# Nine unused tiles that shift the others in SBUF, in a fused attention and bilinear-GLU block

## The chip, the cores and the metric

One NeuronCore of a Trainium2 chip runs the whole program. The metric is the device time of one execution in microseconds; a kernel's time is the median of several executions.

## The reference, cut to what matters

```python
# S = 2048 tokens, D = 576, H = 32 heads of Dh = 18, F = 4608, everything float32
def _A_ref(x, wq, wk, wv, wo):            # 32 query heads, one shared key and value head
    q = (x @ wq).reshape(B, S, H, Dh).transpose(0, 2, 1, 3)
    k, v = x @ wk, x @ wv
    p = softmax(einsum("bhqd,bkd->bhqk", q, k) * Dh ** -0.5)
    return einsum("bhqk,bkd->bhqd", p, v).transpose(0, 2, 1, 3).reshape(B, S, H * Dh) @ wo
def _B_ref(x, w_gate, w_up, w_down):      # bilinear GLU, no nonlinearity
    return ((x @ w_gate) * (x @ w_up)) @ w_down
h  = x + _A_ref(layernorm(x), wq, wk, wv, wo)
h2 = h + _B_ref(layernorm(h), w_gate, w_up, w_down)
```

## The kernel before, in words

The 2048 tokens are four blocks of 512 (`NB`, `TB`). Almost every product is built from float32r matmuls: an operand is split into a high part and the rest (`split`: a cast on one engine and a subtraction on another), and a product is the sum of high by high, high by low and low by high.

*First stage, to about 300 us.* `keys_values` normalises x, transposes it into `XT` (nine chunks of 512 columns per block), and makes keys (`kT`), values (`V`) and the queries. Queries go through DRAM (`q_dram`) and come back four heads at a time as a tile `q`.

*Attention.* `pair` issues one pair of score matmuls (line 593): keys of 128 positions are the weights, 512 queries are the moving operand; the two matmuls of a pair use the partitions 0 to 55 and 64 to 119 at the same time. ScalarE takes the exponential of the pair's 1024 columns into a tile `P` (line 594). `flush` then issues the four matmuls of `P` with `V` (line 598), which are plain float32 and appear as eight instructions.

*Feed-forward stage, from about 360 us.* `ffn(b)` runs over 36 slices of the hidden width for each token block. A slice has 27 pairs of matmuls (line 986): the gate and the up product run at the same time on the two halves of the partitions. Their weights are slices of `ws`, 128 columns each, and their moving operand is a chunk of `X`, 512 columns. While attention for a later block is still to be done (token blocks 0 and 1), a score pair is put in front of every fourth pair (`j % 4 == 0`) and the outputs are called `pg` and `pu`. In token blocks 2 and 3 no scores are left and the output is called `gu`. Every second slice is followed by `down` (line 946): 42 matmuls whose weights are 128-column slices of `room` and whose moving operand is 288 columns of `wdo`; they form a seven-product scheme over two hidden slices.

*Loads.* `load_w` loads the weights of a slice into `wr`, 4608 bytes per partition. `split_w` (line 852) splits them into one of two `ws` tiles of 9216 bytes and loads the slice after next. `load_wd` loads `wdo`.

*Where tiles lie in SBUF.* Pools lie one after another in the order in which they are opened, a pool's tiles in the order of their first use, and each size is rounded up to 32 bytes. So a tile's address is the sum of what is in front of it. In this kernel all chunk steps along the operands of lines 593, 946 and 986 are multiples of 128 bytes, so that all matmuls of a line see the same remainder of their address by 128. TensorE executes its instructions in the order in which the program lists them (`manual_schedule`), and no order depends on an address.

Of the kernel before, what the change touches and what calls it, by code (L numbers as in the profile page):

```python
# [17 lines left out]
F32 = mybir.dt.float32  # L18
# [7 lines left out]
P = 128  # L26
# [28 lines left out]
class Block:  # L55
# [796 lines left out]
    def split_w(self, n):  # L852
        if n < NF * NB:
            r = self.wr.pop(n)
            w = self.ws[n] = self.wp.tile([P, 2, 9, P], F32R, tag="ws", bufs=2, name=f"ws{n}")
            self.split(w[:, 0], w[:, 1], r, self.nc.gpsimd.tensor_copy)
            self.load_w(n + 2)

# [297 lines left out]
    def run(self):  # L1156
        from contextlib import ExitStack
        tc = self.tc
        self.q_dram = tc.dram_tile([NB, H * DH, 3, TB], F32, name="q_dram")
        self.wd_dram = tc.dram_tile([NC, P, 7, 2, HD], F32, name="wd_dram")  # L1160
        self.m_dram = tc.dram_tile([NB, 2, H, TB], F32, name="m_dram")
        self.known, self.n_mx = [0] * NB, 0
        self.tqs, self.p2 = [], None
        self.begin(True)
        with ExitStack() as st:
            pool = lambda name, bufs, **k: st.enter_context(tc.tile_pool(name=name, bufs=bufs, **k))
            cp, self.lp, self.hp = pool("const", 1), pool("ln", 2), pool("resid", 2)
            self.qp, self.pp, self.op, self.otp = pool("q", 2), pool("P", P_BUFS), pool("o", 1), pool("oT", 1)
            self.ps, self.w0 = pool("ps", 1, space=PSUM), pool("w0", 3)
            self.C = cp.tile([P, C_W], F32, name="C")  # L1170
            self.ident = self.C[:, C_ID:C_ID + P]
            self.kT = cp.tile([P, S], F32R, name="kT")
            self.V = cp.tile([P, NT, 32], F32, name="V")
            self.G = cp.tile([P, 64], F32R, name="G")
            self.mx = cp.tile([H, 8], F32, name="mx")
            st.enter_context(tc.manual_schedule())
            with tc.tile_pool(name="p0q", bufs=1) as self.p0q:
                self.wq_h = self.p0q.tile([P, 5, 28 * DH], F32R, name="wq_h")
                self.wq_l = self.p0q.tile([P, 5, 28 * DH], F32R, name="wq_l")
                self.kvq = self.p0q.tile([P, NB, TB], F32, name="kvq")  # L1180
                self.XT = [self.p0q.tile([P, 9, TB], F32R, tag=f"XT{b}", name=f"XT{b}") for b in range(NB)]
                with tc.tile_pool(name="qb", bufs=2) as self.qb:
                    def rest():
                        for b in range(1, NB):
                            yield from self.queries(b)
                    others = rest()
                    self.keys_values(others)
                    self.cast = self.dve.tensor_copy
                    live, due = True, 0.0
                    while live:  # L1190
                        if self.n_pair >= WO_FROM and not self.wo_r0:
                            for c in range(3):
                                self.load_wo_0(c)
                        self.pair()
                        due += RATE
                        while due > 0 and live:
                            z = next(others, None)
                            live = z is not None
                            due -= z or 0
                        self.pair()  # L1200
                        self.run_aux(1)
                        self.flush(len(self.pend) - 1)
            self.wp, self.hh, self.p2 = pool("w", 2), pool("hid", 4), pool("P2", 1)
            self.blocks()
            self.guard()
# [141 lines left out]
```

## Time and profile before

| | |
|---|---|
| median of 3 runs | 2293.43 us (2293.05 to 2294.3) |
| profiled execution: its time, its span | 2291.9 us, 2290.4 us |
| TensorE (PE) busy | 2268.7 us, 99% of the span |
| weight loads (PEld) busy | 1599.6 us, 70% |
| ScalarE (ACT), VectorE (DVE), GpSimd (POOL) busy | 1436.5, 1180.3, 681.3 us |
| granted TensorE clock | 0.999 |

The span runs from the first to the last instruction; the profiled execution's time is 1.5 us longer than its span, and 1.5 us shorter than the median of the runs. In the rows of the profile "64\*128 64x512" are the rows and columns of the array that a matmul uses and the shape of its moving operand. In the view of one line's instructions, three numbers with slashes are the minimum, the median and the maximum duration of one instruction in ns. A matmul's duration is longer than the distance to the next one, since matmuls are pipelined.

### The profile page before, as it was taken

Reading aid. Unit: us, or ns where it says so; the run is one execution under the profiler, and the core shown is the slowest. Engines: PE = TensorE matmul, PEld = TensorE weight load, DVE = VectorE, ACT = ScalarE, POOL = GpSimd, SP = SyncE. Lnnn points to the kernel's source line nnn. Section 1 sums busy time; section 2 is a strip of 40 time slices with the busy share of each in tenths; the row PEclk is TensorE's granted clock in tenths of the full one; section 3 lists DMA queues with packets and bytes.
Section 4 is the critical chain, followed back from the end, with each engine's and each line's share of the span. In section 5 each row is a group of like instructions: output and inputs, shape, how many; then the busy total and the mean of one; then the engine's idle time right before and its main releaser. Section 6 shows DMA issues by size and latency. Waiting matters only on the chain.

```text
span 2290.4 us, 45926 instructions
## 1 busy us (share of the span) xinstructions
PE 2268.7 (99%) x18114; PEld 1599.6 (70%) x18114; DVE 1180.3 (52%) x2152; ACT 1436.5 (63%) x1877; POOL 681.3 (30%) x856
## 2 busy tenths in 40 slices
PE   8999999999999999999999999999999999999998
PEld 6333346677777767677767677777767788888987
DVE  8232435565656567343434355444444476566665
ACT  5889887776676666767666767667677623232332
POOL 4000003455554444122221222222122233333342
PEclk9999999999999999999999999999999999999999
DMA  5222304434333344533333343633333354655553
GB/s 176 81 75 73 111 30 136 148 139 151 136 122 128 136 159 137 207 115 122 113 114 105 125 128 125 192 125 120 98 118 118 120 173 171 213 171 171 179 186 109
DMA packets 127129, 306.75 MB, mean 134 GB/s; under 512 B 17553, under 2 KB 17681, under 8 KB 126265
## 3 DMA queue, kind: packets, MB, share of 16 engines
q1 hardware_dynamic: 126905, 303.73, 39.8%
q8 instruction: 145, 2.38, 0.4%
q14 instruction: 79, 0.65, 0.1%
HBM read 233.76 MB, written 55.67 MB: 126 GB/s over the span
## 4 chain that ended last, share of the span: by engine, by line


## 5 line engine op out<-in xcount | busy, mean ns | idle before, releaser
L594 ACT ACTIVATE P<-s 128x1024 f32<-128x1024 f32 x1024 | 1024.0, 1026 | 271.4 <-PE s L593 189.6
L986 PE MATMUL pg<-X,ws 64*128 64x512 f32 x2592 | 706.9, 391 | 0.0
L986 PE MATMUL pu<-X,ws 64*128 64x512 f32 x2592 | 706.7, 391 | 0.1
L986 PEld LDWEIGHTS pg<-X,ws 64*128 64x128 f32 x2592 | 480.2, 186 | 75.9 <-issue 1.2
L986 PEld LDWEIGHTS pu<-X,ws 64*128 64x128 f32 x2592 | 478.1, 186 | 19.1 <-DVE h L751 1.0
L598 PE MATMUL acc<-P,V 128*32 128x512 f32 x4096 | 487.9, 598 | 0.0
L593 PE MATMUL s<-q,kT 56*128 56x512 f32 x2048 | 455.3, 423 | 5.2 <-ACT P L594 3.3
L946 PEld LDWEIGHTS y<-wdo,room 128*128 128x128 f32 x2856 | 386.9, 188 | 46.7 <-issue 44.2
L946 PE MATMUL y<-wdo,room 128*128 128x288 f32 x2856 | 403.7, 300 | 0.0
L953 ACT COPY tmp<-y 128x288 f32<-128x288 f32 x408 | 162.7, 399 | 330.8 <-PE y L946 313.2
L593 PEld LDWEIGHTS s<-q,kT 56*128 56x128 f32 x2048 | 208.1, 184 | 199.4 <-ACT P L594 118.3
L986 PE MATMUL gu<-X,ws 64*128 64x512 f32 x2592 | 301.8, 389 | 0.5 <-DMA X<-X 0.5
L954 POOL TENSOR_TENSOR x<-x,tmp 128x288 f32<-128x288 f32 x204 | 159.1, 810 | 446.2 <-ACT tmp L953 445.7
L598 PEld LDWEIGHTS acc<-P,V 128*32 128x32 f32 x4096 | 114.0, 109 | 242.5 <-issue 231.1
L986 PEld LDWEIGHTS gu<-X,ws 64*128 64x128 f32 x2592 | 247.6, 184 | 48.8 <-issue 4.8
L88 POOL CAST ws<-wr 128x1152 fp32r<-128x1152 f32 x144 | 170.9, 1187 | 325.6 <-PE pu L986 176.2
L954 POOL TENSOR_TENSOR h<-h,tmp 128x288 f32<-128x288 f32 x204 | 159.1, 810 | 345.8 <-ACT tmp L953 345.6
L89 DVE TENSOR_TENSOR ws<-wr,ws 128x1152 fp32r<-128x1152 f32 x144 | 199.1, 1383 | 74.7 <-POOL ws L88 74.7
L1020 DVE TENSOR_TENSOR hf<-pu,g 128x512 f32<-128x512 f32 x96 | 66.3, 691 | 269.0 <-ACT g L1016 265.6
L949 DVE TENSOR_TENSOR x<-x,y 128x288 f32<-128x288 f32 x272 | 117.7, 452 | 145.6 <-PE y L946 145.6
L949 DVE TENSOR_TENSOR h<-h,y 128x288 f32<-128x288 f32 x272 | 118.4, 454 | 111.8 <-PE y L946 109.8
L89 DVE TENSOR_TENSOR room<-S,room 128x1024 fp32r<-128x1024 f32 x68 | 85.1, 1251 | 147.7 <-ACT room L88 147.7
(172 smaller groups left out, 1621.9 us busy)
## 6 DMA issues: line engine op xcount, KB each, us to landing
wdo<-wd_dram SPq DMA_DIRECT2D x369, 288.0 KB
wr<-in_wgu_dram SPq DMA_DIRECT2D x144, 576.0 KB
wd_dram<-wdo SPq DMA_DIRECT2D x123, 288.0 KB
q<-q_dram SPq DMA_DIRECT2D x64, 216.0 KB
raw<-in_wd_dram SPq DMA_DIRECT2D x36, 288.0 KB
q_dram<-qs SPq DMA_DIRECT2D x15, 504.0 KB
X<-X SPq DMA_DIRECT2D x24, 256.0 KB
ob<-ob SPq DMA_DIRECT2D x121, 36.0 KB
```

What stands on the lines that cost most here:

```text
L88: (copy or self.cast)(hi, src)
L89: self.dve.tensor_tensor(lo, src, f32(hi), ALU.subtract)
L593: self.pe.matmul(s_[:, i], self.kT[o:o + 56, t * P:(t + 1) * P], q[o:o + 56, pr], start=True, stop=True)
L594: self.act.activation(p_, s_, AF.Exp, scale=SCALE)
L598: self.pe.matmul(acc[32 * j:32 * j + 32, :], self.V[:, t, :], Ps[j // 2][:, j % 2, :], start=(t == 0), stop=(t == NT - 1), skip_group_chec ...
L946: pe.matmul(y[:, :HD], m[:, t * P:(t + 1) * P], k, start=(first and j == 0), stop=(j == 2), skip_group_check=True)
L949: dve.tensor_tensor(hs, hs, y[:, :HD], ALU.add)
L953: act.copy(z, y[:, :HD])
L954: pool.tensor_tensor(hs, hs, z, ALU.add)
L986: pe.matmul(ps, w[o:o + 64, wk, c], X[o:o + 64, xk, c], start=(j == 0), stop=(j == 26))
L1020: dve.tensor_tensor(hf, pu, g, ALU.mult)
```

## The change

Nine tiles are allocated that nothing writes or reads. Each takes 32, 64 or 96 bytes of every partition and moves what lies behind it. `gap1` and `gap2` stand on both sides of `kT` and together take 128 bytes, so `kT` alone moves against its neighbours; `gap3` and `gap4` do the same around the two `q` tiles, `gap5` and `gap6` around the two `ws` tiles. `gap` moves everything behind the constants by 64 bytes, and `gap0` everything behind the pool `w0` by 96 more. No instruction is added, removed or reordered, and no tile changes its size.

```diff
     def split_w(self, n):
         if n < NF * NB:
             r = self.wr.pop(n)
+            if n == 0:
+                self.wp.tile([P, 8], F32, tag="gap5", bufs=1, name="gap5")
             w = self.ws[n] = self.wp.tile([P, 2, 9, P], F32R, tag="ws", bufs=2, name=f"ws{n}")
+            if n == 0:
+                self.wp.tile([P, 24], F32, tag="gap6", bufs=1, name="gap6")
             self.split(w[:, 0], w[:, 1], r, self.nc.gpsimd.tensor_copy)
...
             self.ident = self.C[:, C_ID:C_ID + P]
+            cp.tile([P, 8], F32, name="gap1")
             self.kT = cp.tile([P, S], F32R, name="kT")
+            cp.tile([P, 24], F32, name="gap2")
             self.V = cp.tile([P, NT, 32], F32, name="V")
             self.G = cp.tile([P, 64], F32R, name="G")
             self.mx = cp.tile([H, 8], F32, name="mx")
+            self.qp.tile([P, 8], F32, tag="gap3", bufs=1, name="gap3")
+            self.pp.tile([P, 24], F32, tag="gap4", bufs=1, name="gap4")
+            cp.tile([P, 16], F32, name="gap")
+            self.w0.tile([P, 24], F32, tag="gap0", bufs=1, name="gap0")
```

Adding up the sizes gives the remainders of the addresses by 128 bytes:

| tile | used as | before | after |
|---|---|---|---|
| `kT` | weights of the scores | 0 | 32 |
| `q` | moving operand of the scores | 64 | 32 |
| `X` | moving operand of gate and up | 0 | 32 |
| `ws` | weights of gate and up | 0 | 64 |
| `wdo` | moving operand of `down` | 0 | 32 |
| `room` (`oT`) | weights of `down` and of the output projection | 96 | 32 |
| `wos` | moving operand of the output projection | 0 | 32 |
| `XT` | moving operand of the first projections | 64 | 96 |
| `wq_h`, `wq_l` | weights of the query projections | 0, 96 | 32, 0 |
| `P`, `V` | moving operand and weights of line 598 | 64, 0 | 0, 0 |
| `wr` | landing place of the gate and up weights | 0 | 32 |
| `h`, `ob` | residual rows, attention output | 64 | 0 |
| `g`, `hf`, `S`, `tmp` | small tiles of the feed-forward stage | 0 | 32 |

## The prediction

> **What bounds the kernel now.** I read the page's busy times first, then TensorE's groups, then who TensorE waited for, then the durations inside its lines, and last the order of time in two stretches.
>
> ```profile
> PE 2268.7 (99%) x18114; PEld 1599.6 (70%) x18114; DVE 1180.3 (52%) x2152; ACT 1436.5 (63%) x1877; POOL 681.3 (30%) x856
> ```
>
> ```profile
> PE warm L307 <- DMA C<-in_cst_dram: 6.3, 1, 6.3
> PE s L593 <- ACT P L594: 3.3, 11, 0.4
> ...
> PE gu L986 <- DMA X<-X: 0.5, 1, 0.5
> ```
>
> TensorE is busy for 99% of the span, and its waits are small: 6.3 us once at the start for a load, 3.3 us on ScalarE, 0.5 us on one transfer. No other engine and no transfer sets the end. So only a change in the pace of TensorE's own matmuls can move the time, and since the change adds and removes no instruction, the question is whether that pace depends on where the operands lie.
>
> ```profile
> L986 PE MATMUL pg<-X,ws 64*128 64x512 f32 x2592 | 706.9, 391 | 0.0
> L986 PE MATMUL pu<-X,ws 64*128 64x512 f32 x2592 | 706.7, 391 | 0.1
> ...
> L598 PE MATMUL acc<-P,V 128*32 128x512 f32 x4096 | 487.9, 598 | 0.0
> L593 PE MATMUL s<-q,kT 56*128 56x512 f32 x2048 | 455.3, 423 | 5.2 <-ACT P L594 3.3 <-DVE XT L89 1.8
> ...
> L946 PE MATMUL y<-wdo,room 128*128 128x288 f32 x2856 | 403.7, 300 | 0.0
> ...
> L986 PE MATMUL gu<-X,ws 64*128 64x512 f32 x2592 | 301.8, 389 | 0.5 <-DMA X<-X 0.5
> ```
>
> These six rows are nearly all of TensorE's time. Two matmuls of line 986 or 593 run side by side, so there are 2592 pairs of pg and pu, 1296 pairs of gu and 1024 score pairs.
>
> Now the same lines one instruction at a time (minimum, median, maximum in ns):
>
> ```profile
> L593 PE MATMUL s<-q,kT x2048: 385/397/507, 35.8 to 1822.0; 56*128 56x512 f32 x187
> L986 PE MATMUL pg<-X,ws x2592: 383/392/502, 359.4 to 1821.7; 64*128 64x512 f32 x200
> ...
> L986 PE MATMUL gu<-X,ws x2592: 383/386/502, 1825.9 to 2276.2; 64*128 64x512 f32 x200
> L946 PE MATMUL y<-wdo,room x2856: 290/297/404, 396.3 to 2269.9; 128*128 128x288 f32 x191
> L598 PE MATMUL acc<-P,V x4096: 592/592/617, 43.7 to 1825.3; 128*32 128x512 f32 x196
> L233 PE MATMUL psk<-XT,wk x56: 387/397/480, 14.5 to 61.2; 128*108 128x512 f32 x56
> ```
>
> All these matmuls but line 598's and 946's stream the same 512 columns, at the same granted clock, yet gu has a median of 386 ns, pg 392 and the scores 397. Something lengthens them by up to 11 ns, and it is not the length of the work. The float32 passes of line 598 show nothing of it: minimum and median are both 592. In order of time it looks like this:
>
> ```profile
> 1201.67 0.42 PE L593 MATMUL s<-q,kT 56*128 56x512 f32 x2
> 1201.91 0.39 PE L986 MATMUL pg<-X,ws 64*128 64x512 f32 x1
> ...
> 1202.14 0.39 PE L986 MATMUL pg<-X,ws 64*128 64x512 f32 x1
> ...
> 1202.84 0.41 PE L593 MATMUL s<-q,kT 56*128 56x512 f32 x2
> ...
> 1204.00 0.42 PE L593 MATMUL s<-q,kT 56*128 56x512 f32 x2
> ...
> 1205.15 0.42 PE L593 MATMUL s<-q,kT 56*128 56x512 f32 x2
> ```
>
> From 1201.67 to 1205.15 there are three score pairs, each followed by four pairs of line 986: 15 pairs in 3.48 us, 232 ns a pair. The score pair itself takes 0.24 us until the next pg, the first pg pair 0.23. Where no scores are left, in the later blocks, the matmuls run evenly:
>
> ```profile
> 1996.69 3.11 PE L986 MATMUL gu<-X,ws 64*128 64x512 f32 x26
> ```
>
> These are 13 pairs. The last one ends 386 ns after its start, so 12 distances take 3.11 - 0.386 = 2.72 us: 227 ns a pair. The even run is thus 5 ns a pair better than the mixed one, and the disturbance enters with the score pair.
>
> What differs there? By the remainders in the table of the change, X and ws both lie at 0, and the even run belongs to them. The queries lie at 64 and the keys at 0, and during a score pair the next weights (ws, at 0) are being loaded. Line 233 fits: its moving operand XT lies at 64 too, and its median is 397, as for the scores. That is a hint, and no more, that the moving operand's place, or its distance to the weights loaded meanwhile, costs up to 11 ns of a matmul.
>
> **The change part by part.**
>
> *Instructions, queues, waits.* The unused tiles are never written, so no engine and no queue gets anything more. All places move by the same bytes in every partition. Cost: nothing, with nothing that would have to hide it.
>
> *Queries, keys, X and gate/up weights (lines 593 and 986).* The moving operands q and X come to the same remainder, 32. The distance from the moving operand to the weights loaded meanwhile becomes 32 bytes for X with ws (0 before) and for q with ws (64 before), and stays 0 for X with kT. So the score pair no longer differs from its neighbours as it did. What is there to gain is the distance of the mixed run from the even run: 2592 pairs of pg and pu, and a score pair to every four of them, 648, are 3240 pairs of 232 - 227 = 5 ns, 16.2 us in all. I can't see in any row what a distance of 32 bytes does, so the bounds are: all of it gained, -16.2 us; or the even run lost, which is priced under the rivals. I take half of the gain, -8.1 us, because of the two things that set the score pair apart (another place of the moving operand, another distance) the change removes the first fully and the second in part.
>
> *Down projection (line 946).* wdo goes from 0 to 32 and room from 96 to 32, so that moving operand and weights get the distance 0, which before belongs to X with ws. Its median lies 7 ns above its minimum (297 against 290), where gu at distance 0 lies 3 above (386 against 383). If line 946 came as close, it would gain 4 ns in 2856 matmuls, 11.4 us; all 7 would be 20.0 us. Since its neighbours differ in a fixed order of three and it has 288 columns instead of 512, I take half of 4: 2 ns, -5.7 us.
>
> *Scores outside the feed-forward stage, first projections, output projection.* 1024 - 648 = 376 score pairs stand beside line 598 and other matmuls; at 11 ns (397 against 386) they are worth 4.1 us either way, and XT's 56 matmuls of line 233 far less. Nothing says which way, and I set them at 0.
>
> *P and V (line 598).* P goes from 64 to 0. Its durations do not vary (592/592), though the further tiles for it in the pool P2 lie at 0 before already. Cost 0.
>
> *Transfers.* wr, wdo and X now land at 32 instead of 0, the queries at 32 instead of 64.
>
> ```profile
> 1996.70:2001.60 4.90, 4.90 (x46) 4.07 (x44) 1.00 0.84 284
> ```
>
> This row (line 986's busy times in a stretch of the last blocks: PE, PEld, clock, share of the DMA engines' time, GB/s) shows TensorE without a gap at a DMA share of 0.84. The transfers have some room even in their densest stretch, and TensorE's waits on them are 0.5 us after the start. I set the new landing places at 0; were they a fifth slower, that share would reach 1 and the weights' arrival would begin to count, which lies inside the range.
>
> *Sum.* -8.1 - 5.7 = -13.8 us. Against the profiled execution's 2291.9 us that is 2278.1; the median of the runs lies 1.5 us above that execution, so 2279.6 us, 0.6% faster.
>
> **The rivals.**
>
> *Nothing moves.* Places do not matter to the matmuls, and the 386, 392 and 397 ns come from what stands in line behind what: a score pair uses 56 of 64 rows, carries the waits of the exponential, and upsets the stream wherever its operands lie. For it: pg and gu use the same tiles at the same places and still differ by 6 ns. Against it: line 233 carries no exponential, uses all 128 rows, and also has 397. Then every row stays: 2293.4 us. [...]
>
> *The even run is lost.* The 227 ns of gu may hang on X and ws having the same remainder; at a distance of 32 bytes each gu pair could settle at the pace of the mixed run. That is 1296 x 5 = 6.5 us more. If the new distance is as bad as that of the scores, gu goes from 386 to 397, 1296 x 11 = 14.3 us, and the pg pairs from 392 to 397, 2592 x 5 = 13.0 us: 27.3 us more. It decides from the point where gu's median leaves 386 by more than 5 ns without the scores improving by as much. Half-way, some 13 us more, it gives 2306 us. For it: gu's 386 is the best median of all the 512-column float32r lines, so a new place has more to lose there than to gain. Against it: the scores' place is the worst, and has as much to gain.
>
> **How the numbers follow.** The forecast gets 0.50, nothing moves 0.17, the even run lost 0.33. A difference of 0.2%, 4.6 us, is about what a measurement of this kernel tells from no change; a little of the forecast's case falls inside it, and a little of the second rival's, as gains and losses may cancel: faster 0.48, same 0.20, slower 0.32. The range takes in the forecast with both gains nearly full (16.2 + 11.4 = 27.6 us, 2265.8) and the slower rival a little past its half-way point: 2264 to 2308. The forecast's own range is 2264 to 2288.
>
> **What would show it.** Right, step by step: the score matmuls' median falls from 397 towards 390, pg's and pu's from 392 towards 388, 15 pairs of the mixed run take 3.43 us or less instead of 3.48, gu stays at 386, and line 946's median falls from 297 to 295. Line 598 stays at 592. Wrong: gu's median above 386; a mixed run of 3.48 us or more; new waits of TensorE on wr, wdo or X, which would mean that the landing places cost something. If all medians stay, the first rival holds.

## The result, and the profile after

| | before | after |
|---|---|---|
| median of 8 runs each, taken together | 2293.43 us (2291.57 to 2294.3) | 2299.64 us (2298.68 to 2300.26) |
| profiled execution: its time, its span | 2291.9, 2290.4 us | 2300.26, 2298.5 us |

The ratio is 1.0028, with a 95% interval of 1.002 to 1.0036. The kernel got some 6 us slower where 2279.6 us, a gain of 14 us, was forecast. The sign was wrong; the time lies inside the range of 2264 to 2308. In the kernel after, lines behind 854 have moved by four: 986 is now 990, and 946 is 950.

The page of the kernel after, busy times of the engines and the large groups of TensorE:

```profile
PE 2276.4 (99%) x18114; PEld 1588.1 (69%) x18114; DVE 1180.7 (51%) x2152; ACT 1436.3 (62%) x1877; POOL 680.9 (30%) x856
...
L990 PE MATMUL pg<-X,ws 64*128 64x512 f32 x2592 | 709.8, 392 | 0.1
L990 PE MATMUL pu<-X,ws 64*128 64x512 f32 x2592 | 709.2, 392 | 0.1
...
L598 PE MATMUL acc<-P,V 128*32 128x512 f32 x4096 | 487.7, 598 | 0.0
L593 PE MATMUL s<-q,kT 56*128 56x512 f32 x2048 | 450.1, 421 | 5.2 <-ACT P L594 3.2 <-DVE XT L89 1.8
...
L950 PE MATMUL y<-wdo,room 128*128 128x288 f32 x2856 | 403.4, 300 | 0.0
...
L990 PE MATMUL gu<-X,ws 64*128 64x512 f32 x2592 | 309.6, 394 | 0.6 <-DMA X<-X 0.6
```

TensorE is still busy for 99% of the span, with 7.7 us more busy time than before (2276.4 against 2268.7) for the same instructions. One group carries it: gu rose from 301.8 to 309.6 us, 7.8 us. The scores fell from 455.3 to 450.1, and pg and pu, which run side by side, rose by 2.9 and 2.5.

TensorE's waits after:

```profile
PE warm L307 <- DMA C<-in_cst_dram: 7.6, 1, 7.6
...
PE s L593 <- ACT P L594: 3.2, 11, 0.4
...
PE gu L990 <- DMA X<-X: 0.6, 1, 0.6
```

No wait took the place of another. The first load came 1.3 us later in this one execution than in that of before (7.6 against 6.3). That is 1.3 of the 1.9 us by which the spans' difference (8.1 us) is over that of the medians (6.2); the rest is not accounted for.

The views of single lines: minimum, median and maximum in ns, then the first and the last start in us.

```profile
L593 PE MATMUL s<-q,kT x2048: 383/393/506, 37.1 to 1822.9; 56*128 56x512 f32 x187
L990 PE MATMUL pg<-X,ws x2592: 384/392/502, 360.5 to 1822.7; 64*128 64x512 f32 x200
L990 PE MATMUL gu<-X,ws x2592: 387/392/500, 1826.8 to 2284.9; 64*128 64x512 f32 x200
L950 PE MATMUL y<-wdo,room x2856: 287/296/407, 397.3 to 2278.5; 128*128 128x288 f32 x191
```

Two stretches can be read off the last numbers, and they are the measure for all experiments below. The **mixed stretch**, from the first pg to the last, took 1462.3 us before (359.4 to 1821.7) and takes 1462.2 us after. The **last stretch**, from the first gu to the last, took 450.3 us before (1825.9 to 2276.2) and takes 458.1 us: 7.8 us more. So the loss lies behind 1826 us, where no scores are left, and the mixed stretch, in which 8.1 us were to be gained, did not move. (The last stretch is the last 48 slices, 1296 pairs; the first 24 slices of token block 2 still have scores in them, which the description of the kernel leaves out.)

The order of time shows the pace. First the score pairs of the mixed run of the kernel after, with four pairs of line 990 between two of them:

```profile
1202.79 0.39 PE L593 MATMUL s<-q,kT 56*128 56x512 f32 x2
...
1203.95 0.39 PE L593 MATMUL s<-q,kT 56*128 56x512 f32 x2
...
1205.11 0.40 PE L593 MATMUL s<-q,kT 56*128 56x512 f32 x2
...
1206.27 0.40 PE L593 MATMUL s<-q,kT 56*128 56x512 f32 x2
```

15 pairs take 3.48 us, 232 ns a pair, to the digit what they took before. Then two slices of gu in one piece, 54 pairs, in the kernel before and in the kernel after:

```profile
2032.06 12.53 PE L986 MATMUL gu<-X,ws 64*128 64x512 f32 x108
```

```profile
2036.34 12.86 PE L990 MATMUL gu<-X,ws 64*128 64x512 f32 x108
```

They take 0.33 us more, which is 6 ns for each of 54 pairs, and the last stretch holds 24 such pieces: 7.9 us, all that it lost. In start times the pairs of an undisturbed slice lie 227, 227, 226 ns apart before, and between 230 and 236 after.

### The profile page after: what moved, and what is told of

Same layout as the page of the kernel before. It is cut to its first block, busy times and chain, and to the rows that moved or that the text cites. A ratio compares the mean times of both kernels' runs of the same rounds, so it can differ in the third digit from the quotient of the medians.

```text
span 2298.5 us, 45926 instructions
## 1 busy us (share of the span) xinstructions
PE 2276.4 (99%) x18114; PEld 1588.1 (69%) x18114; DVE 1180.7 (51%) x2152; ACT 1436.3 (62%) x1877; POOL 680.9 (30%) x856
## 4 chain that ended last, share of the span: by engine, by line
PE 95%; DVE 1%; ACT 1%; DMA 1%; issue 1%; SPq 0%; POOL 0%; ACTq 0%; DVEq 0%
PE acc L598 20%; PE y L950 17%; PE pg L990 16%; PE gu L990 13%; PE s L593 12%; PE pu L990 10%; PE yo L750 3%; PE psq L445 2%; ACT P L594 1%; PE y L908 1%; DMA X<-X 1%; PE psk L233 0%; DVE XT L89 0%; PE ye L908 0%; PE tx L819 0%
## 5 line engine op out<-in xcount | busy, mean ns | idle before, releaser
L593 PE MATMUL s<-q,kT 56*128 56x512 f32 x2048 | 450.1, 421 | 5.2 <-ACT P L594 3.2
L950 PE MATMUL y<-wdo,room 128*128 128x288 f32 x2856 | 403.4, 300 | 0.0
L990 PE MATMUL gu<-X,ws 64*128 64x512 f32 x2592 | 309.6, 394 | 0.6 <-DMA X<-X 0.6
```

The lines of the kernel that those rows point to most:

```text
L593: self.pe.matmul(s_[:, i], self.kT[o:o + 56, t * P:(t + 1) * P], q[o:o + 56, pr], start=True, stop=True)
L950: pe.matmul(y[:, :HD], m[:, t * P:(t + 1) * P], k, start=(first and j == 0), stop=(j == 2), skip_group_check=True)
L990: pe.matmul(ps, w[o:o + 64, wk, c], X[o:o + 64, xk, c], start=(j == 0), stop=(j == 26))
```

## The experiments

Two theories were stated first. **D**: a pair's pace hangs on the distance, in address, from the moving operand to the weights that are loaded during it. **M**: it hangs on the place of the moving operand itself. The table gives every kernel's median, its ratio to the kernel before with the 95% interval, and the two stretches read off the views of single lines as above, in one profiled execution each (before: 1462.3 and 450.3). Where there is no interval, it is one execution. The distance is the address of ws less that of X, by 256 bytes (the scan below shows why by 256).

| kernel | distance | median us | ratio | mixed | last |
|---|---|---|---|---|---|
| after | 32 | 2299.64 | 1.0028 (1.002 to 1.0036) | 1462.2 | 458.1 |
| e1_ws32 | 32 | 2301.95 | 1.0039 (1.0026 to 1.0053) | 1463.7 | 458.7 |
| e2_ws64 | 64 | 2306.51 | 1.0058 (1.0044 to 1.0072) | 1467.7 | 458.0 |
| e5_ws96 | 96 | 2308.2 | 1.0069 (1.0055 to 1.0082) | 1468.6 | 459.2 |
| e8_ws16 | 16, 144 | 2299.81 | 1.0032 (1.002 to 1.0044) | 1461.8 | 458.0 |
| e3_q0 | 0 | 2294.41 | 1.0007 (0.9998 to 1.0016) | 1464.4 | 449.5 |
| e6_q96 | 0 | 2295.46 | 1.0012 (1.0003 to 1.0021) | 1464.8 | 449.9 |
| e7_room0 | 0 | 2295.83 | 1.0016 (1.0007 to 1.0025) | 1465.8 | 449.2 |
| e4_w32 | 0 | 2293.62 | 1.0003 (0.9994 to 1.0012) | 1462.4 | 450.5 |
| e16_change_ws_back | 0 | 2294.53 | 1.0006 (0.9997 to 1.0015) | 1463.8 | 450.3 |
| e12_all512 | 0 | 2291.48 | 0.9995 (0.9986 to 1.0004) | 1461.7 | 450.0 |
| e13_gu56 | 0 | 2299.04 | | 1462.2 | 457.7 |
| e14_rows64 | 0 | 2287.89 | 0.998 (0.9971 to 0.9989) | 1457.5 | 450.0 |
| e15_rows64_equal | 0 | 2282.39 | 0.9955 (0.9942 to 0.9969) | 1452.7 | 449.8 |
| e17_rows64_change | 32 | 2300.22 | 1.0029 (1.0017 to 1.0041) | 1461.7 | 457.7 |
| e18_rows64_wdo | 0 | 2283.88 | 0.9959 (0.9945 to 0.9972) | 1453.0 | 450.0 |

### One part of the change alone: ws moved, nothing else in the mixed run

```diff
-            w = self.ws[n] = self.wp.tile([P, 2, 9, P], F32R, tag="ws", bufs=2, name=f"ws{n}")
+            _ = n == 0 and self.wp.tile([P, 8], F32, tag="ga", bufs=1, name="ga")
+            w = self.ws[n] = self.wp.tile([P, 2, 9, P], F32R, tag="ws", bufs=2, name=f"ws{n}")
+            _ = n == 0 and self.wp.tile([P, 24], F32, tag="gb", bufs=1, name="gb")
```

e1 has 8 and 24 elements of 4 bytes, e2 has 16 and 16, e5 has 24 and 8. X, q and kT stay where they are.

> Only the two ws tiles move, from 0 to 32 by 128 bytes; X stays at 0, so the distance from the moving operand to the weights loaded meanwhile is 32, as in the change. Theory D (the distance counts): gu goes from a median of 386 to about 394 as in the change, 1296 pairs x some 6 to 8 ns, about 2301 us; the scores change too, since their distance to ws goes from -64 to -32. Theory M (the moving operand's own place counts): X is where it was, so gu stays at 386, the scores at 397 and the time at 2293.4. Theory R (something else that the change moved, such as P, room or wdo): gu stays at 386.

> Only ws moves, to 64; X at 0, distance 64 for the gate and up pairs, 0 for queries with ws. Theory D: gu leaves 386 again (the scores of before, with a distance of 64, have 397; so up to 1296 x 11 = 14 us more), and the scores fall from 397 to about 390, 1024 x 7 = 7 us less: between 2293 and 2308 us. Theory M: all medians as before, 2293.4 us.

> Only ws moves, to 96; X at 0: the last of the four distances. Gu ran at 227 ns a pair at distance 0 and at 233 at 32 and at 64. Theory D4 (four places by 128 bytes, and only the same place is good): 233 ns at 96 too, 1296 x 6 = 8 us more, plus what the mixed run does, about 2301 us. Theory D- (the order of the places counts, one step behind is best): gu below 227, 1296 x some 5 ns less, about 2287 us.

The line of gu in e1:

```profile
L986 PE MATMUL gu<-X,ws x2592: 386/392/501, 1827.8 to 2286.5; 64*128 64x512 f32 x200
```

The last stretch is 458.7 us, as after the whole change, while X stands where it stood before. The two tiles around ws are enough for the loss. At 64 and 96 bytes the last stretch is much the same (458.0, 459.2), but the mixed stretch loses 5 to 6 us as well. In e2 the scores were to fall to about 390 ns, since queries and ws then have the same remainder by 128; they stayed at 398.

### The counter-test: X and ws moved together

```diff
             self.mx = cp.tile([H, 8], F32, name="mx")
+            self.w0.tile([P, 8], F32, tag="gh", bufs=1, name="gh")
```

In e4 this moves the whole weight pool, X and ws with it, by 32 bytes. e16 is the whole change without `gap5` and `gap6`: X and ws both come to 32.

> The whole pool of the feed-forward stage moves by 32: X, ws, wdo, wr, wos and the small tiles are at 32, the distance from X to ws is 0 again, kT stays at 0, q at 64, room at 96. Theory D: gu stays at 386 although X is at 32; line 946 has a distance of 64 instead of 96 and may move either way; 2288 to 2300 us. Theory M: gu goes to 394 as in the change, 1296 x 6 to 8 ns, about 2301 us.

> The change without gap5 and gap6: X and ws both at 32, distance 0, queries and keys at 32 as in the change. Theory D: gu is back at 227 ns, 1296 x 6 = 8 us less than the change, and 0 to 2 us less than before for line 950's pace (134.0 ns in the change): 2291 to 2294 us. If something else of the change slowed gu: 2299.6.

The line of gu in e4 and in e16:

```profile
L986 PE MATMUL gu<-X,ws x2592: 383/386/503, 1827.0 to 2277.5; 64*128 64x512 f32 x200
```

```profile
L986 PE MATMUL gu<-X,ws x2592: 383/386/501, 1829.0 to 2279.3; 64*128 64x512 f32 x200
```

X lies at 32 by 128 bytes as after the change (in e16 at the very address), and gu has its 386 ns and its 450 us again. M says that the place of X decides, and falls; D stands. What lies behind ws moves by 128 bytes in e1, e2 and e5, so that these runs alone leave it as a rival; the scan below moves ws inside its own tile, and gu's pace follows it from slice to slice. e16 differs from the change in the two tiles around ws alone and is not to be told from before: the two tiles around ws cost what the change costs. (The change has eight tiles, as its diff shows; the title and the description count nine.)

### Other distances in the mixed run

```diff
+            self.qp.tile([P, 16], F32, tag="ge", bufs=1, name="ge")
+            self.pp.tile([P, 16], F32, tag="gf", bufs=1, name="gf")
```

e3 puts these in front of q and behind it, so that q comes to 0; e6 has 8 and 24 and brings q to 96. e7 moves `oT` and `room` to 0:

```diff
+            self.otp.tile([P, 8], F32, tag="gi", bufs=1, name="gi")
+            self.w0.tile([P, 24], F32, tag="gj", bufs=1, name="gj")
```

Each adds 128 bytes in all.

> Only the two query tiles move, from 64 to 0; everything else is as before, gate and up pairs at distance 0. Theories D and M both: scores fall from 397 to near 386 to 390, and the pg and pu pairs behind them run more evenly (392 to 389): 1024 x 7 + 2592 x 3 ns = up to 15 us less, 2278 us; gu stays at 386. If the score pair upsets the stream wherever the queries lie (the rows of the array or the waits), 2293.4 us and 397 stay.

> Only the queries move, from 64 to 96; X, ws and kT stay at 0, so queries to ws have a distance of 32, as in the change, where the score pair's own distance to the next pair fell from 235.6 to 231.6 ns, while X keeps distance 0. Theory D, each pair by itself: score pairs gain 4 ns and the rest of the mixed run stays, 1024 x 4 = 4 us less, 2289 us, and gu stays at 227. Theory H (the run behind a score pair hangs on how the score pair ended, so that a gain in one place of the five is given back in the others, as with the queries at 0): the 15 pairs of the mixed run stay within 1% of 3.48 us and the time between 2291 and 2297.

> Only room (and oT) moves, from 96 to 0, with wdo at 0: distance 0 between the two operands of line 946, as in the change. If the change's gain on line 946 (134.7 to 134.0 ns a matmul) comes from that distance, it shows here alone: 2856 x 0.65 = 1.9 us less, 2291.5 us. As forecast in the prediction it would be 2856 x 2 = 5.7 us less, 2287.7. If the distance is nothing to line 946: 2293.4.

None of the gains came. e3 is not to be told from before, though its scores' median fell from 397 to 393. e6 lies where its Theory H put it: the scores' median fell from 397 to 392 ns, and the mixed stretch got no shorter for it (1464.8 us). e7 misses all its figures: line 946's busy time fell from 403.7 to 402.9 us, 0.8 us, and the kernel got slower. The last stretch keeps its 450 us, but the mixed stretch gets 2 to 4 us longer, e7's although neither q, kT, X nor ws changes its remainder by 128. What does change in all three is that X and ws stand 128 bytes further from kT and, in e7, from q. That 128 bytes were taken for nothing was a mistake of these experiments, and of the table of the change, whose remainders are by 128; the scan shows why. By 256 the change itself moves X and kT 128 bytes against each other (416 bytes are put in front of X, 32 in front of kT), where the prediction has their distance stay at 0.

### The scan: another distance in every slice

```diff
-            w = self.ws[n] = self.wp.tile([P, 2, 9, P], F32R, tag="ws", bufs=2, name=f"ws{n}")
+            o = n % NF % 36 * 16
+            w = self.ws[n] = self.wp.tile([P, 2880], F32R, tag="ws", bufs=2, name=f"ws{n}")[:, o:o + 2304].rearrange("p (k c m) -> p k c m", k=2, c=9)
```

e10 takes steps of 64 bytes and two tiles of 45 x 256 bytes; e9 takes steps of 4 bytes and tiles 128 bytes more than a multiple of 256. e8 is one place alone, 16 bytes in, also with tiles of that size, so that its second tile is at 144. e9 (2302.73 us) and e10 (2300.45 us) were run once.

> ws starts 16 bytes inside a longer tile; X at 0: a distance of 16 bytes, a step that the change cannot make. If places are 32 bytes wide and both operands still share most of a place, gu stays near 227 or settles between, 230 (2293 to 2298 us); if any distance breaks the even run, 233 ns and about 2302 us.

> Each hidden slice f puts its ws f mod 32 elements (of 4 bytes) further inside a longer tile, so that the slices of the blocks without scores show the pace of the gu pairs at every distance from 0 to 124 bytes in steps of 4. [...] Theory E (any distance breaks the even run): 227 at 0 alone. Theory G (some other distance is better still): a slice with less than 227. The time itself says little, about 2300 us.

> The same in steps of 64 bytes, 0 to 2240. If only the remainder by 128 counts, every second slice runs at 227 ns a pair and the others at 233. If the period is 256 or 512, every fourth or eighth; that would explain why the mixed run changed when room, wdo, X and ws were moved by multiples of 128 against keys and queries (235 ns a pair instead of 232 with room at 0).

Four slices of e10 in order of time, 20 pairs of each; the distances are 64, 128, 192 and 0 by 256:

```profile
2187.33 4.83 PE L986 MATMUL gu<-X,ws 64*128 64x512 f32 x40
```

```profile
2193.62 4.82 PE L986 MATMUL gu<-X,ws 64*128 64x512 f32 x40
```

```profile
2205.97 4.74 PE L986 MATMUL gu<-X,ws 64*128 64x512 f32 x40
```

```profile
2212.16 4.70 PE L986 MATMUL gu<-X,ws 64*128 64x512 f32 x40
```

Less the 0.39 us by which the last pair outlasts its start, these are 19 distances: 234, 233, 229 and 227 ns a pair. From start times, over more of the slice, it is 233, 232, 229 and 226.7, and it repeats with every 256 bytes: the slices at 0, 256, 512 and 768 all settle at 226.7, those at 128, 384, 640 and 896 all at some 232.4. So a distance of 128 bytes is not one of 0. In e9's slices of the last token block, 16, 120 and 132 have 226.7 as 0 has, 8 and 24 have some 231, 40 to 112 have 232.0 to 234.4, and from 140 up (156 apart) all lie between 231 and 238. No distance tried goes below 226.6, and the slices of the kernel before already settle at 226.6 to 226.7.

e8 adds a warning. Its first slice of the last block, at 16 bytes, runs at 227, the later ones at the same 16 bytes at 233.3, behind slices at 144; and its very last slice, at 144, runs at 226.7, where all the others at 144 have 233. In e9 the slice at 156 goes at 226.7 for 13 pairs and then at some 243, and the slice at 32 behind it at 267 for most of its length, where e1 has 233.3 at 32. So at some distances the pace also hangs on what ran before. With 64 rows in all gu pairs, no slice at 0 stayed at a slow pace in any run: the last stretch is 449.2 to 450.5 us in all these kernels.

### What upsets the mixed run

No place tried so far brought the mixed run below its 232 ns. Two reasons were left: the score pair's operands stand at other distances, or it is the score pair as such, which uses 56 of 64 rows.

```diff
             self.mx = cp.tile([H, 8], F32, name="mx")
+            self.qp.tile([P, 16], F32, tag="ge", bufs=1, name="ge")
+            self.otp.tile([P, 24], F32, tag="gi", bufs=1, name="gi")
+            self.w0.tile([P, 24], F32, tag="gh", bufs=1, name="gh")
```

By the sizes in front of them, e12 brings kT, q, X, ws, wdo and room to the same remainder by 512, so that every distance of the mixed run is 0.

> Keys, queries, X, ws, wdo and room all get the same remainder by 512 (384), by 64 bytes in front of the queries, 96 more in front of room and 96 more in front of X; keys stay. Theory D512 (distances count by 512, and a score pair upsets the run because its distances differ from X to ws): the score pair no longer differs, the mixed run goes from 232 towards 227 ns a pair: 3240 x 5 = up to 16 us less, 2277 us. Theory H (the score pair upsets the run by its rows or waits): the mixed run stays at 232 ns, 2293 us; gu at 227 in both.

```profile
L986 PE MATMUL pg<-X,ws x2592: 383/392/498, 360.6 to 1822.3; 64*128 64x512 f32 x200
```

The mixed stretch is 1461.7 us against 1462.3. With all these distances at 0 next to nothing is gained.

```diff
-                        pe.matmul(ps, w[o:o + 64, wk, c], X[o:o + 64, xk, c], start=(j == 0), stop=(j == 26))
+                        r = 56 if not on and j % 4 == 3 else 64
+                        pe.matmul(ps, w[o:o + r, wk, c], X[o:o + r, xk, c], start=(j == 0), stop=(j == 26))
```

> In the token blocks without scores every fourth gu pair uses 56 of its 64 rows (8 rows of the contraction are left out there), with the places of before. Theory K (a pair with fewer rows upsets the run): gu leaves 227 ns a pair for about 231 to 233, 1296 x 5 = 6 us more. Theory S (the waits or the other tiles of a score pair do it): gu stays at 227.

e13 puts what is left into the even run, with ws and X at distance 0, and nothing but the rows of some pairs changed (the kernel leaves out 8 rows of the contraction there). Its groups by shape, and two slices in one piece:

```profile
L986 PE MATMUL gu<-X,ws 64*128 64x512 f32 x2016 | 293.2, 395 | 0.4 <-DMA X<-X 0.4
...
L986 PE MATMUL gu<-X,ws 56*128 56x512 f32 x576 | 120.3, 392 | 0.0
```

```profile
2035.02 12.85 PE L986 MATMUL gu<-X,ws 64*128 64x512 f32 x108
```

288 pairs with fewer rows make all 1296 slower: 12.85 us for 54 pairs instead of 12.53, and a last stretch of 457.7 us. Pairs with 56 rows among pairs with 64 are enough to upset a run; no run has pairs with 56 rows alone. The opposite is to give the score pairs 64 rows:

```diff
+        _ = [self.nc.gpsimd.memset(f32(q[o:o + 32]), 0.0) for o in (32, 96)]
...
-            self.pe.matmul(s_[:, i], self.kT[o:o + 56, t * P:(t + 1) * P], q[o:o + 56, pr], start=True, stop=True)
+            self.pe.matmul(s_[:, i], self.kT[o:o + 64, t * P:(t + 1) * P], q[o:o + 64, pr], start=True, stop=True)
```

The added rows of q are zero. e14 has this alone; e15 has it with e12's places; e17 has it with the change; e18 is e15 with the two halves of `wdo` 1280 bytes apart instead of 1152.

> The score pairs use 64 rows, the 8 added ones hold zeros in the queries (two fills on GpSimd for each q tile); places as before. Theory K: the score pairs still have queries at 64, so the mixed run gains in part, 230 ns a pair: 3240 x 2 = 6 us less, 2287 us. Theory S: 232 ns stays, 2293 us or a little more for the fills.

> 64 rows as above, and keys, queries, X, ws, wdo and room at the same remainder by 512, as in e12. Theory K: nothing sets a score pair apart any more, the mixed run goes to 227 ns a pair, 3240 x 5 = 16 us less, 2277 us. Theory S: as e12, 2292 us.

> All nine unused tiles of the change, and score pairs of 64 rows. Theory D: X and ws at a distance of 32 run at 233 ns a pair everywhere, so that the 64 rows bring nothing on the mixed run: 232 to 233 ns a pair there, gu 233, about 2299 us, some 17 us over the 64-row kernel with equal places. If the distance only mattered in the blocks without scores: mixed run 228, 2290 us.

> The kernel of e15 with the halves of each wdo tile 1280 bytes apart instead of 1152, so that both lie at the place of room by 256. If line 946 hangs on the distance as gu does, its matmuls settle at 133.3 ns: 2856 x 1 = 3 us less than e15, 2279.5 us. If it does not, 2282.4; the loads of wdo in two pieces per partition may cost, where a transfer comes late.

The line of pg in e14:

```profile
L986 PE MATMUL pg<-X,ws x2592: 383/386/500, 359.5 to 1817.0; 64*128 64x512 f32 x200
```

Single lines of e15, and its score pairs in the order of time:

```profile
L593 PE MATMUL s<-q,kT x2048: 383/386/507, 37.3 to 1813.6; 64*128 64x512 f32 x187
```

```profile
L986 PE MATMUL pg<-X,ws x2592: 383/386/502, 360.7 to 1813.4; 64*128 64x512 f32 x200
...
L986 PE MATMUL gu<-X,ws x2592: 383/386/501, 1817.5 to 2267.3; 64*128 64x512 f32 x200
```

```profile
1201.12 0.40 PE L593 MATMUL s<-q,kT 64*128 64x512 f32 x2
...
1202.26 0.40 PE L593 MATMUL s<-q,kT 64*128 64x512 f32 x2
...
1203.39 0.40 PE L593 MATMUL s<-q,kT 64*128 64x512 f32 x2
```

In e15 the scores and pg have gu's 386 ns, and 10 pairs take 2.27 us: the mixed run goes at 227. The mixed stretch falls by 9.6 us, where 16 were expected of this run, and the time to 2282.39, the best kernel here. Neither part does it alone: the rows without the places gain 4.8 us of the stretch (e14), the places without the rows 0.6 (e12). With the change's places, where X and ws stand 32 bytes apart, the rows bring nothing:

```profile
L990 PE MATMUL pg<-X,ws x2592: 383/392/502, 360.7 to 1822.4; 64*128 64x512 f32 x200
...
L990 PE MATMUL gu<-X,ws x2592: 388/392/499, 1826.6 to 2284.3; 64*128 64x512 f32 x200
```

That is e17, with 1461.7 and 457.7 us. In this kernel an even pace of the mixed run needs both: pairs that all use the same rows, and distances at which the run comes back to it. The zero fills are hidden: GpSimd's busy time rises from 681.3 to 742.7 us of a span of 2281.0.

### Line 946

```diff
-            w = self.wdo[b, p, j] = self.wp.tile([P, 2, HD], F32R, tag="wdo", bufs=WD_BUFS, name=f"wdo{b}_{p}_{j}")
+            o = p % 16 * 4
+            w = self.wdo[b, p, j] = self.wp.tile([P, 640], F32R, tag="wdo", bufs=WD_BUFS, name=f"wdo{b}_{p}_{j}")[:, o:o + 576].rearrange("p (k d) -> p k d", k=2)
```

> In token blocks 1 to 3 the wdo tiles of the hidden pair p start 16 x (p mod 16) bytes inside their slots; room stays. Line 946 then shows its pace at 16 distances from 0 to 240 bytes. If its pace hangs on the distance as gu's does, some hidden pairs run at 133.3 ns a matmul without spread and the others at 134 to 136; if not, all lie within 134 to 135.

```profile
L946 PE MATMUL y<-wdo,room x2856: 288/296/407, 396.5 to 2269.9; 128*128 128x288 f32 x191
```

e11 (2291.97 us, one execution) moves wdo by another 16 bytes in each step. Every place gives 133 to 135 ns from one matmul to the next (distances over 160 ns left out), and none stands out; e18, which makes all distances equal, has 134.0 too, and its 2283.88 us are no gain on e15. The line's busy time is 403.3 us in e11 and 402.7 in e18, against 403.7 before: none of the places tried is worth more than 1 us to these matmuls of 288 columns.

## Why the prediction was wrong, point by point

*What bounds the kernel: right.* TensorE stayed busy for 99%, and the time moved by the pace of its own matmuls and nothing else. No engine or queue got more to do, P and V kept 592 ns, and with the new landing places of the transfers TensorE's wait on X was 0.6 us, against 0.5.

*Queries, keys, X and gate/up weights: the step that failed.* It went wrong twice. 8.1 us were to be gained in the mixed run, and 0.1 was. And gu, which lost 7.8 us, stood in the sum with nothing (next point). The step took the score pair's place or distance for what sets it apart. The runs show a third thing, its 56 rows: e12 gives it the best distances and gains 0.6 us, and e13 carries the disturbance into the even run with rows alone. The rival "Nothing moves" had named just that ("a score pair uses 56 of 64 rows [...] and upsets the stream wherever its operands lie"), and got a chance of 0.17, with line 233's 397 ns against it, a row of 56 matmuls that use all 128 rows and run in another company. It came true on the mixed run and not on gu, where places decide. Places can help the mixed run too, but only once the rows are equal: they then bring 4.8 us of its stretch (e15 against e14).

One part did come as said. The scores' median fell from 397 to 393, and the time from a score pair to the next pg fell from 235.6 ns to 231.6 (start times, means over undisturbed rounds). But the pairs behind gave it back: the fourth of the round went from 230.3 to 232.7, the last from 228.4 to 229.7, and the five together from 1160.6 to 1160.0. Why is argued from the traces: at a distance of 0 the even run comes back to 227 ns some six pairs after a disturbance, and at 32 it stays at 233. So the change made the disturbance by the score pair a little smaller and took away the recovery.

*The even run is lost: the rival that came true,* and it should have stood in the sum. It was priced at 1296 x 5 = 6.5 us; measured are 6 ns a pair and 7.8 us. Its larger price of 27.3 us did not come: gu went to 392 and not to 397, and pg from 392 to 392. At 32 bytes the mixed run, which is upset anyway, had nothing to lose; at 64 and 96 it did lose 5 to 6 us (e2, e5). The text gave this case 0.33 and wrote beside it that gu "has more to lose there than to gain", yet the sum let gu stand at 386 under the very distance that it counted as a gain elsewhere. That is a contradiction which could be seen without a run: the change put 32 bytes where the one fast run of the kernel had 0.

*Down projection: the size was off.* 5.7 us were forecast; the line's busy time fell from 403.7 to 403.4 us, 0.3 us. Where the matmuls follow each other without a longer stop (distances below 160 ns), the mean distance did fall from 134.69 ns to 134.04, which would be 1.9 us in 2856 matmuls, but the distances of 160 ns and more rose from 86 to 128 in number and took most of it back. The 4 ns were read off the gap between median and minimum, and e11 and e18 show no place that closes it.

*Weights loaded beside the matmul.* The prediction could not see in any row what a distance of 32 bytes between X and ws does. In e1 the move of ws alone, by 32 bytes, with X where it was, took two slices of gu from 12.53 to 12.86 us, 6 ns for each of 54 pairs: here the place of the weights counts for the matmuls. The scan, in which ws moves inside its own tile, shows the same (233 ns a pair at 64, 226.7 at 0).

*What would show it.* gu's median above 386 and a mixed run of 3.48 us were named as the signs of a wrong forecast, and both are there. That the time lies inside the range is owed to the slower rival, which the range takes in, and not to the forecast.

**What stays open.** Why a distance matters, why it repeats with 256 bytes, and why pairs of 56 rows upset the run, no run here shows. The trace suggests why a few score pairs cost so much: in the kernel before, the pairs at the head of a slice that follows `down` mostly lie 231, 236, 228, 233, 230 and only then 227 ns apart, and in the mixed run a score pair comes every fifth pair, ahead of that. That was read, not tested.

## What to carry to other kernels

Where the median duration of one matmul form differs between two stretches of the same kernel (386 and 392 ns here), take the even run for something that can be lost, and price it in the sum before counting a gain from an operand that is moved. For pairs like these, keep the distance from the moving operand to the next weights at a multiple of 256 bytes (226.7 ns a pair here, against 229 to 234 at 32, 64, 96, 128 and 192), and measure any other; then look at whether neighbouring matmuls use the same number of rows, since filling up rows with zeros brought 0.45% here together with the places, and less than half of it alone. A shift of 128 bytes is not neutral (232.4 ns a pair in e10), so a control that "moves nothing" has to keep the address by 256.

## What the runs showed of the hardware that was not expected

- Pairs of float32r matmuls of 512 columns on the two halves of the rows run at 226.7 ns a pair at a distance of 0 by 256 bytes, at 233 at 32 and 64, at 234 at 96, at 232 at 128 and at 229 at 192 (after, e1, e2, e5, e10); no slice settled below that.
- At 16 and at 144 bytes both paces were seen, 226.7 and 233, behind different slices (e8, e9); at 32 bytes 233.3 (e1) and, in one slice, 267 (e9).
- 576 matmuls on 56 rows among 2592 made the whole stretch 7.4 us longer (450.3 to 457.7), about as much as a distance of 32 to 96 bytes did (458.0 to 459.2).
- Equal rows and equal distances gain little alone, 4.8 and 0.6 us of the mixed stretch, and 9.6 us together.
